# Token softmax sums kept as rows, their inverses spread through DRAM, token outputs divided on GpSimd one segment later

## The chip, the cores and the metric

One core of one Trainium2 chip runs the whole program. The metric is the device time in microseconds (us), the median of some runs of the same kernel. One more execution is taken under the profiler; all durations below come from that one.

## The reference, cut to what matters

Two layers, each an attention block A with a recurrent memory and a gated block B. The change is in A. The sequence of 2048 tokens is cut into 64 segments of 32, and each segment's first 8 output rows are the memory of the next, so the segments of a block follow one another strictly.

```python
for s in range(n_seg):                       # 64 segments, S = 2048, seg_len = 32
    h = concatenate([mem, xs])               # 8 memory rows and 32 tokens, Dm = 512
    q, k, v = (einsum('btd,dhe->bhte', h, W) for W in (Wq, Wk, Wv))   # 32 heads of 128
    scores = where(mask, einsum('bhqe,bhke->bhqk', q, k) * scale, -1e9)
    p = softmax(scores)                      # every query has its own sum over the keys
    o = einsum('bhqk,bhke->bhqe', p, v)
    o = einsum('bhte,hed->btd', o, Wo)
    mem = o[:, :M]                           # M = 8: wanted by the next segment
    outs.append(o[:, M:])                    # wanted only at the end of the block
```

The kernel works without a maximum: it takes exp of the scaled scores, multiplies by a mask of 0 and 1, and divides the product with V by the sum.

## The kernel before, in words

`a_block` (from L657) runs 64 times the function `segment` (from L891); 128 segments in the two layers. In one segment, in the order in which the code hands work to the engines:

- **Projections.** `qk` (L905) makes q and k in four chunks of 16 matmuls (L701), `v_mm` makes v in two. ScalarE casts each chunk to bf16 (L908), VectorE transposes it (L911) into `QQ` (queries) and `KA` (keys, two buffers in turn). The last 8 tokens of each segment don't depend on the memory; their q, k and v come a block of 128 tokens ahead, from the filler described below, and GpSimd copies them into `QQ` and `KX` (`prep_segment`, L864 and L867), a segment or more before they are read.
- **Scores.** `scores(r)` (L934, L938) for each half r of the heads, `exps(r)` on ScalarE (L943), `close(r)` on VectorE (L946), which multiplies `S` by the mask into `E`. Between the two, VectorE copies the second half of V out of PSUM (`VA`, L1040).
- **Sums and products.** `sums_ahead` (L969) sums the memory queries of half 0 over the keys, `pv(r)` (L986, L989) multiplies `E` by V into `psO`, `sums_memory` (L960) sums the memory queries of half 1, and `sums_tokens` (L978) those of the 32 tokens. `sums_tokens` and `sums_memory` use a matrix of ones 128 wide as weights, so that each sum stands in all 128 partitions at once: `psT` is 128 x 1024. `memory_out(r)` inverts the memory sums on ScalarE as exp(-ln) (L1003, L1004), and VectorE multiplies (L1005) into `uT`, columns 24 to 31.
- **Output projection.** `wo_pairs` (`px`, L777) and `wo_rest` (L784) multiply `uT` of this segment, 32 columns for each head, by Wo. Columns 24 to 31 are this segment's memory rows, columns 0 to 23 the first 24 token rows of the segment before: `tok_out` put them there. So the token outputs are wanted by the `px` of the next segment. The last 8 token rows go to `oB` (`last_out`) and are projected blocks later.
- **The way back.** ScalarE and VectorE copy one part of `px` (`cross`, L1065 and L873), VectorE adds (L875, L882) and transposes (L883) the memory rows into `hT`; then the next segment's projections can start.
- **Token outputs.** ScalarE inverts `psT` into `Rt` (Ln of 1024 elements, L1067, then Exp twice 512, L1070); VectorE multiplies `psO` by `Rt` in `tok_out` (L1008) and `last_out` (L1011).

The order on TensorE, VectorE and ScalarE is that of the code. GpSimd and SyncE (SP) aren't in that list: their instructions are placed by a scheduler. SP issues the DMAs and does so in order: a DMA that waits holds up those behind it.

**Filler.** `fill()` takes the next piece of work that no segment waits for: the projections of the block to come (`b_units`, L740) or the projection of finished last rows (`y_part`, L800). One unit is 16 matmuls of 512 columns; every second unit is given out in pieces, the others at once. Before the change there are three calls in a segment: one ahead of `sums_ahead` (4 matmuls), one behind it (12), and one near the segment's end (a whole unit), in front of the next projections. In the fourth segment of the first blocks no unit is left and `fill` does nothing.

**Buffers and names that the change touches:** `KAr` (L712) and the pool `a_vs` of `VA` (L679) have two buffers each; `attO` is the PSUM of `psO`, taken again by the next segment's `psK`; `att` that of `psT`, taken again by `psQ`. `spare1` (L1134) and its like hold VectorE and GpSimd work of the rows that are finished.

Of the kernel before, what the change touches and what calls it, by code (L numbers as in the profile page):

```python
# [10 lines left out]
ALU = mybir.AluOpType  # L11
# [42 lines left out]
def _consts(ctx, tc, c, b_sp):  # L54
    nc = tc.nc
    cp = ctx.enter_context(tc.tile_pool(name="consts", bufs=1))
    bsp = cp.tile([P, 16], F32, name="bsp")
    tctx = ExitStack()
    tmp = tctx.enter_context(tc.tile_pool(name="consts_tmp", bufs=1))
    ident_f = tmp.tile([P, P], F32, name="ident_f")  # L60
    nc.gpsimd.memset(ident_f[:], 0.0)
    nc.gpsimd.affine_select(out=ident_f[:], in_=ident_f[:], compare_op=ALU.not_equal, fill=1.0,
                            base=0, pattern=[[-1, P]], channel_multiplier=1)
    ident_bf = cp.tile([P, P], BF16, name="ident_bf")
    nc.vector.tensor_copy(ident_bf[:], ident_f[:])
# [24 lines left out]
    nc.vector.memset(ones[:], 1.0)  # L90
    half = cp.tile([P, 2, 32], BF16, name="half")
    nc.vector.memset(half[:], 0.0)
    for g in range(2):
        nc.vector.memset(half[64 * g:64 * g + 64, g, :], 1.0)
    bsp_bf = cp.tile([P, 16], BF16, name="bsp_bf")
# [8 lines left out]
    c.update(ident_bf=ident_bf, maskN=maskN, ones=ones, half=half)  # L104
    return c


# [374 lines left out]
def kernel(  # L482
# [30 lines left out]
    rp = ctx.enter_context(tc.tile_pool(name="rows", bufs=1))  # L513
    rows = _Rows(nc, rp, xd, xb_d, o_d, x_in)
    rows.vb_d = dram.tile([P, 8 * DH], BF16, name="vb_d")
    with tc.manual_schedule(engines=ORDERED):
        _act_table(nc)
        for tt in range(2):
# [138 lines left out]
def a_block(tc, c, rows, front, MV_in, RS_in, MV_out, RS_out, ahead, wo, S, first):  # L657
# [1 line left out]
    NSEG = S // SEG  # L659
    NB = S // P  # L660
    scale = float(DH) ** -0.5
    maskN, ones, half = c["maskN"], c["ones"], c["half"]

    with ExitStack() as ctx:

# [10 lines left out]
            KTBr[i], QTBr[i] = (a.rearrange("p (r h k) -> p r h k", r=2, h=16) for a in v[2:])  # L676
        pers = ctx.enter_context(tc.tile_pool(name="a_pers", bufs=1))
        wk = ctx.enter_context(tc.tile_pool(name="a_work", bufs=2))
        vsp = ctx.enter_context(tc.tile_pool(name="a_vs", bufs=2))  # L679
        rowp = ctx.enter_context(tc.tile_pool(name="a_rows", bufs=4))  # L680
        segp = ctx.enter_context(tc.tile_pool(name="a_seg", bufs=2))
        acc_pool = ctx.enter_context(tc.tile_pool(name="a_ps_acc", bufs=1, space=PSUM))
# [26 lines left out]

        memT = [pers.tile([P, P], BF16, name=f"memT{i}") for i in range(2)]  # L710
        NKQ = 2
        KAr = [pers.tile([P, 2, 16, 32], BF16, name=f"KA{i}") for i in range(2)]  # L712
        QQr = [pers.tile([P, 2, 16, 40], BF16, name=f"QQ{i}") for i in range(NKQ)]
        KXr = [pers.tile([P, 4, 2, 32], BF16, name=f"KX{i}") for i in range(NKQ)]
        uT = [pers.tile([P, H, 32], BF16, name=f"uT{i}") for i in range(2)]
# [24 lines left out]
        def b_units(tb, early=0):  # L740
# [59 lines left out]
        def y_part(G, q, last=False):  # L800
# [5 lines left out]
                parts = [[(groups[g], 8 * q + k) for g in range(4)] for k in range(8)]  # L806
            pwB = accA.tile([P, DM], F32, name="pwB")
            for k, _ in enumerate(wo_last(parts, pwB)):
                if k in (0, 3):
                    yield  # L810

            def add(lo, n, src):
# [43 lines left out]

        seg_state = {}
        oBs = {}

        def prep_segment(s, eng=nc.gpsimd):  # L860
            tb, j4 = s // 4, s % 4
# [29 lines left out]
        def segment(s, fill, spare1, spare2, spare3, tail, loads):  # L891
            tb, j4 = s // 4, s % 4
            st = seg_state.pop(s)
            QQ, KX, VX = st["QQ"], st["KX"], st["VX"]
            KA = KAr[s % 2]
# [76 lines left out]
            def sums_tokens(ps):  # L972

                for k in range(2):
                    for g in range(2):
# [2 lines left out]
                        nc.tensor.matmul(o[:, :, :, 24:32] if k else o, lhsT=ones[64 * g:64 * g + 64, :],  # L978
                                         rhs=e_own(e, 1) if k else e_all(e, 8, 40), start=(k == 0), stop=True, skip_group_check=True)

            def pv(r):

                for i in range(4):
# [83 lines left out]
            nc.scalar.activation(out=Rt[:], in_=psT[:], func=ACT.Ln)  # L1067
            for r in range(2):
                rt = Rt[:, :, 256 * r:256 * r + 256]
                nc.scalar.activation(out=rt, in_=rt, func=ACT.Exp, scale=-1.0)  # L1070
            run(turns)
            spare2()
            t1 = wk.tile([P, P], F32, name="t1", bufs=1)
# [10 lines left out]
            tok_out(1)  # L1084
            last_out(1)
            run(adds)
            run(turns)
            tail()
# [4 lines left out]
        if first:  # L1093
# [1 line left out]
                ln_turn(tb, nc.scalar.copy)  # L1095
            units, units1 = b_units(0, 6), b_units(1, 2)
            for gen in (units, units1, units):
                for _ in range(3):
# [13 lines left out]
            rows.y_load(y, first, nc.gpsimd, rows.pool.tile([P, DM], F32, name="y_x")[:], o)()  # L1112

        def values(units):
            for n in (2, 1):
                for _ in range(n):
                    next(units)
                run(copies)
# [152 lines left out]
```

## Time and profile before

| what | value |
|---|---|
| runs | 1626.39, 1627.11, 1627.98 us; median 1627.11 |
| profiled execution, span | 1630.2 us (no other time is given for it) |
| granted TensorE clock, mean | 0.996 |
| one ordinary segment, `scores(0)` to `scores(0)` (309.83 to 319.83) | 10.00 us |
| a segment without filler (119.48 to 129.27) | 9.79 us |
| mean distance of segments, first layer, second layer | 10.09, 10.08 us |
| `sums_tokens` (L978), one segment, from the first start to the last end | 0.44 us |
| `Rt` on ScalarE (L1067, L1070), one segment | 1.02 and 2 x 0.62 us |
| `tok_out`, `last_out` on VectorE (L1008, L1011), one segment | 2 x 0.55 and 2 x 0.28 us |
| DMA moved | 149.27 MB, 92 GB/s on the mean |

How to read it: a row of the order of time gives start, time, engine, line, operation and the tiles "out<-in", and in brackets the idle time before it with what ended it. A row's time reaches from the first start to the last end of a run of equal instructions, and for TensorE the ends are modelled; what can be compared well are the starts. "SPq" and "POOLq" are the queues on which SP and GpSimd issue DMAs.

### The profile page before, as it was taken

The page shows a single profiled execution, that of the slowest core. Times are in us where ns is not written, and L with a number is a line of the kernel's source. Part 1 is how long each engine was busy: PE and PEld are TensorE (multiplying, and loading weights), DVE is VectorE, ACT ScalarE, POOL GpSimd, SP SyncE. Part 2 cuts the span into 40 slices and gives each one's busy share as a digit, 9 for nine tenths or more (in the row PEclk, how much of TensorE's full clock was granted, in tenths as well). Part 3 has the DMA queues.
Part 4 walks back from the last instruction along what each step waited for, and adds up shares of the span by engine and source line. Part 5 has one row for each costly group of instructions (what it writes and reads, how often), then busy time and mean ns, then how long its engine had stood idle before and what let it go on. Part 6 is the DMA issues. An engine that isn't in the chain of part 4 may idle for free.

```text
span 1630.2 us, 90461 instructions
## 1 busy us (share of the span) xinstructions
PE 1575.0 (97%) x40658; PEld 962.0 (59%) x40658; DVE 1211.3 (74%) x3179; ACT 1064.1 (65%) x2278; POOL 290.2 (18%) x604
## 2 busy tenths in 40 slices
PE   4899999999999999999999999999999999999999
PEld 1456665665566556566656566666655666664565
DVE  3677777778888888884467777777888788878622
ACT  2577777777777777661047777777777777775400
POOL 5111111111211221320011111111121112224000
PEclk9899999999999999999999999999999999999999
DMA  9322122223321334387951222121233123425697
GB/s 352 105 44 43 44 44 44 43 46 75 81 56 43 79 87 84 91 182 145 214 167 48 45 50 46 46 46 46 62 97 79 46 72 95 98 55 172 141 189 162
DMA packets 264748, 149.27 MB, mean 92 GB/s; under 512 B 198680, under 2 KB 240784, under 8 KB 264360
## 3 DMA queue, kind: packets, MB, share of 16 engines
q1 hardware_dynamic: 251128, 99.66, 28.4%
q0 software_dynamic: 13232, 43.82, 8.3%
q8 instruction: 319, 5.23, 1.4%
q14 instruction: 69, 0.57, 0.1%
HBM read 59.68 MB, written 37.19 MB: 59 GB/s over the span
## 4 chain that ended last, share of the span: by engine, by line
PE 54%; DVE 1%; ACT 1%; DMA 1%; issue 0%; SPq 0%; DVEq 0%
PE pg L392 9%; PE psQ L701 7%; PE psK L701 7%; PE psb L701 5%; PE pz L291 4%; PE px L777 4%; PE psV L701 3%; PE psm L701 3%; PE psO L784 3%; PE py L435 2%; PE psO L986 2%; PE pwB L796 1%; PE psT L978 1%; PE psS L934 1%; PE pw L1223 0%; PE psO L969 0%
## 5 line engine op out<-in xcount | busy, mean ns | idle before, releaser
L701 PEld LDWEIGHTS <-hT 128*32 128x32 bf16 x12288 | 331.9, 97 | 309.2 <-DVE hT L883 65.5
L911 DVE STREAM_TRANSPOSE QQ<-rows 128x512 bf16<-128x512 bf16 x256 | 179.2, 700 | 20.2 <-ACT rows L908 13.0
L911 DVE STREAM_TRANSPOSE KA<-rows 128x512 bf16<-128x512 bf16 x256 | 176.3, 689 | 14.7 <-ACT rows L908 13.1
L908 ACT CAST rows<-psQ 128x512 bf16<-128x512 f32 x256 | 142.8, 584 | 22.7 <-PE psQ L701 21.1
L392 PE MATMUL pg<-z,wspT 128*128 128x344 bf16 x1024 | 154.3, 309 | 0.0
L1005 DVE TENSOR_TENSOR uT<-psO,Rm 128x128 bf16<-128x128 f32 x256 | 74.5, 291 | 106.7 <-PE psO L989 56.6
L1070 ACT ACTIVATE Rt<-Rt 128x512 f32<-128x512 f32 x256 | 147.3, 622 | 4.1
L1008 DVE TENSOR_TENSOR uT<-psO,Rt 128x384 bf16<-128x384 f32 x256 | 140.4, 548 | 10.8 <-ACT Rt L1070 4.1
L701 PE MATMUL psQ<-Wq_sb,hT 128*32 128x512 bf16 x2048 | 136.2, 383 | 10.2 <-ACT Rt L1067 4.4
L943 ACT ACTIVATE S<-psS 128x224 bf16<-128x224 f32 x256 | 91.4, 357 | 81.1 <-PE psS L938 81.1
L777 PEld LDWEIGHTS <-uT 128*32 128x32 bf16 x4608 | 111.6, 96 | 46.8 <-DVE uT L1005 32.7
L701 PE MATMUL psQ<-Wk_sb,hT 128*32 128x512 bf16 x2048 | 136.2, 383 | 0.0
L777 PE MATMUL px<-Wo,uT 128*32 128x256 bf16 x3840 | 135.3, 275 | 0.3 <-DVE uT L1005 0.3
L701 PE MATMUL psm<-Wq_sb,hT 128*32 128x512 bf16 x2048 | 134.9, 380 | 0.0
L701 PE MATMUL psK<-Wk_sb,hT 128*32 128x512 bf16 x2048 | 134.4, 379 | 0.0
L701 PE MATMUL psK<-Wv_sb,hT 128*32 128x512 bf16 x2048 | 134.4, 379 | 0.0
L701 PE MATMUL psV<-Wv_sb,hT 128*32 128x512 bf16 x2048 | 133.6, 378 | 0.0
L1067 ACT ACTIVATE Rt<-psT 128x1024 f32<-128x1024 f32 x128 | 131.0, 1024 | 3.1
L784 PE MATMUL psO<-Wo_high,uT 128*32 128x128 bf16 x7168 | 126.9, 220 | 5.9 <-issue 3.3
L392 PEld LDWEIGHTS <-wspT 128*128 128x128 bf16 x1024 | 100.2, 98 | 53.2
L867 POOL COPY KX<-old 128x128 bf16<-128x128 bf16 x128 | 69.1, 550 | 299.3 <-PE psS L938 224.8
L867 POOL COPY KX<-front 128x128 bf16<-128x128 bf16 x126 | 66.6, 548 | 303.9 <-PE psS L938 222.5
(194 smaller groups left out, 2908.2 us busy)
## 6 DMA issues: line engine op xcount, KB each, us to landing
o_d<-o_sb SPq DMA_DIRECT2D x126, 64.0 KB
vb_d<-front SPq DMA_DIRECT2D x30, 256.0 KB
VX<-vb_d SPq DMA_DIRECT2D x120, 64.0 KB
ln_x<-xd SPq DMA_DIRECT2D x26, 256.0 KB
y_o<-o_d POOLq DMA_DIRECT2D x22, 256.0 KB, 3.4
xd<-y_o POOLq DMA_DIRECT2D x22, 256.0 KB, 3.2
Wq_sb<-in_A_Wq_dram POOLq DMA_DIRECT2D x8, 512.0 KB, 9.7
Wk_sb<-in_A_Wk_dram POOLq DMA_DIRECT2D x8, 512.0 KB, 11.1
```

Of the source, the lines that this page charges most:

```text
L392: nc.tensor.matmul(pg[t][:, k, 0:344], lhsT=wsp[t][:, st, :], rhs=z(st, 344 * k, 344 * k + 344), start=(st == 0), stop=(st == NT - 1))
L701: return [nc.tensor.matmul(ps[32 * cg:32 * cg + 32, :], lhsT=lhs(kt, cg), rhs=rhs(kt, cg), start=(kt == 0), stop=(kt == KT - 1), tile_posi ...
L777: nc.tensor.matmul(px[at:at + 32, 0:256], lhsT=lhs[:, h, :], rhs=wo_rhs(h, slice(k + 2, None, -2) if h % 2 else slice(k, None, 2)), start= ...
L784: nc.tensor.matmul(pw[32 * cg:32 * cg + 32, :], lhsT=lhs[:, h, :], rhs=wo_rhs(h, cg), start=False, stop=(h == H - 1), tile_position=(0, 32 ...
L867: eng.tensor_copy(KX[:, :, r].rearrange("p g (k i) -> p i g k", i=4), bs["KTB"][:, r].rearrange("p (i g) k -> p i g k", i=4)[:, :, :, 8 * ...
L908: return r, mms, nc.scalar.copy(r[:], ps)
L911: nc.vector.transpose(out=QQ[:, j % 2, :, 0:32] if j < 2 else KA[:, j % 2], in_=r[:])
L943: return nc.scalar.activation(out=S[:, r], in_=psS[:, r, 0:224], func=ACT.Exp, scale=scale)
L1005: nc.vector.tensor_tensor(out=hview(uT_cur[:], r, 24, 32), in0=oview(r, 0, 8), in1=rm.rearrange("p g (n q) -> p g n q", q=8), op=ALU.mult)
L1008: nc.vector.tensor_tensor(out=hview(uT_nxt[:], r, 0, 24), in0=oview(r, 8, 32), in1=rview(r, 0, 24), op=ALU.mult)
L1067: nc.scalar.activation(out=Rt[:], in_=psT[:], func=ACT.Ln)
L1070: nc.scalar.activation(out=rt, in_=rt, func=ACT.Exp, scale=-1.0)
```

## The change

Except in the last segment of a block, where all stays as it was (`ahead_of` is false):

- `sums_rows` takes the place of `sums_tokens`: for each of four (half, key side) parts of `E`, one matmul for all keys and one for the own ones, with the weights `pick` (128 x 32: 16 equal columns of ones for each half of the partitions), in four column tiles of TensorE. Each sum then stands in 16 partitions and not in 128, and `psT` is used 128 x 128.
- ScalarE inverts these 128 x 128 (`Rr`), SP writes one partition out of each 16 to DRAM (`r_d`, 8 x 128), and two DMAs read it back, copied to all 128 partitions, into `Rt`.
- ScalarE copies `psO` (128 x 512 for each half) into `raw` in SBUF; `tok_out` and `last_out` on VectorE go.
- `norm_tokens` multiplies `raw` by `Rt` in eight products on GpSimd, four with 192 elements a partition into `uT` and four with 64 into `oB`. It is kept in `late` and handed out in the next segment, behind its token sums and ahead of its `px`.
- The divided filler unit comes in three pieces (4, 8 and 4 matmuls), and `fill` is called once more, behind the token sums.
- `KA` and `VA` have one buffer each.

Cut to its core:

```diff
-        vsp = ctx.enter_context(tc.tile_pool(name="a_vs", bufs=2))
+        vsp = ctx.enter_context(tc.tile_pool(name="a_vs", bufs=1))
-        KAr = [pers.tile([P, 2, 16, 32], BF16, name=f"KA{i}") for i in range(2)]
+        KAr = [pers.tile([P, 2, 16, 32], BF16, name="KA")]
-                for kts in (((0,), (1, 2, 3)), ((0, 1, 2, 3),))[k % 2]:
+                for kts in (((0,), (1, 2), (3,)), ((0, 1, 2, 3),))[k % 2]:
+            def sums_rows(ps):
+                for k in range(2):
+                    for q in range(4):
+                        e = E[:, q // 2, q % 2, :]
+                        rhs = e[:, 160:224].rearrange("p (i b e) -> p i b e", i=4, b=2)[:, :, 1, :] if k else heads40(e[:, 0:160])[:, :, 8:40]
+                        o = ps[32 * q:32 * q + 32, :].rearrange("p (i q) -> p i q", i=4)
+                        nc.tensor.matmul(o[:, :, 24:32] if k else o, lhsT=pick[:].rearrange("p g m -> p (g m)"), rhs=rhs,
+                                         start=(k == 0), stop=True, tile_position=(0, 32 * q), skip_group_check=True)
+            def raw_out(raw, r):
+                nc.scalar.copy(raw[:, r].rearrange("p g s i q -> p g (s i) q"), oview(r, 8, 40))
...
-            sums_tokens(psT)
+            ahead_of = s + 1 < NSEG
+            if ahead_of:
+                sums_rows(psT[:, 0, 0:P])
+            else:
+                sums_tokens(psT)
+            if late:
+                late.pop(0)()
+            if not (first and s == 0):
+                fill()
             memory_out(1, sums[1])
...
+            if ahead_of:
+                Rr = segp.tile([P, P], F32, name="Rr", bufs=1)
+                nc.scalar.activation(out=Rr[:], in_=psT[:, 0, 0:P], func=ACT.Ln)
+                nc.scalar.activation(out=Rr[:], in_=Rr[:], func=ACT.Exp, scale=-1.0)
+                r_d = rows.r_d[s % 2]
+                nc.sync.dma_start(r_d[:], Rr[:].rearrange("(a b) c -> a b c", b=16)[:, 0, :])
+                raw = segp.tile([P, 2, 2, 2, 4, 32], F32, name="raw", bufs=1)
+                rb = Rt[:].rearrange("p r (s g i q) -> p r s g i q", s=2, g=2, i=4)
+                for r in range(2):
+                    nc.sync.dma_start(Rt[:, r, :], r_d[4 * r:4 * r + 4, :].rearrange("a c -> (a c)").partition_broadcast(P))
+                    raw_out(raw, r)
+                def norm_tokens():
+                    for lo, hi in ((0, 24), (24, 32)):
+                        for r in range(2):
...
+                            for k in range(2):
+                                nc.gpsimd.tensor_tensor(out=o[:, :, k], in0=raw[:, r, :, k, :, lo:hi], in1=rb[:, r, k, :, :, lo:hi], op=ALU.mult)
+                late.append(norm_tokens)
...
-            tok_out(0)
-            last_out(0)
+            if not ahead_of:
+                tok_out(0)
+                last_out(0)
             fill()
```

More of the change, by code (lines that the diff above doesn't have):

```diff
@@ L94, in _consts @@
         nc.vector.memset(half[64 * g:64 * g + 64, g, :], 1.0)
+    pick = cp.tile([P, 2, 16], BF16, name="pick")
+    nc.vector.memset(pick[:], 0.0)
+    for g in range(2):
+        nc.vector.memset(pick[64 * g:64 * g + 64, g, :], 1.0)
     bsp_bf = cp.tile([P, 16], BF16, name="bsp_bf")
@@ L103, in _consts @@
     tctx.close()
-    c.update(ident_bf=ident_bf, maskN=maskN, ones=ones, half=half)
+    c.update(ident_bf=ident_bf, maskN=maskN, ones=ones, half=half, pick=pick)
     return c
@@ L515 @@
     rows.vb_d = dram.tile([P, 8 * DH], BF16, name="vb_d")
+    rows.r_d = [dram.tile([8, P], F32, name=f"r_d{i}") for i in range(2)]
     with tc.manual_schedule(engines=ORDERED):
@@ L661, in a_block @@
     scale = float(DH) ** -0.5
-    maskN, ones, half = c["maskN"], c["ones"], c["half"]
+    maskN, ones, half, pick = c["maskN"], c["ones"], c["half"], c["pick"]
     with ExitStack() as ctx:
@@ L808, in y_part @@
             for k, _ in enumerate(wo_last(parts, pwB)):
-                if k in (0, 3):
+                if k in (0, 2, 3):
                     yield
@@ L858, in a_block @@
         oBs = {}
+        late = []
         def prep_segment(s, eng=nc.gpsimd):
@@ L894, in segment @@
             QQ, KX, VX = st["QQ"], st["KX"], st["VX"]
-            KA = KAr[s % 2]
+            KA = KAr[0]
             VA = vsp.tile([P, 2, 4, DH], BF16, name="VA")
@@ L1066, in segment @@
             Rt = segp.tile([P, 2, 512], F32, name="Rt", tag="Rt", bufs=1)
[L1067 to L1070, printed above, removed]
+            if ahead_of:
[12 more added lines that the diff above has]
+                        for r in range(2):
+                            if lo == 0:
+                                o = uT_nxt[:, :, 0:24]
+                            else:
+                                o = oB[:, :, 8 * (s % 16):8 * (s % 16) + 8]
+                            o = o.rearrange("p (r g s i) q -> p r g s i q", r=2, g=2, s=2)[:, r]
+                            for k in range(2):
+                                nc.gpsimd.tensor_tensor(out=o[:, :, k], in0=raw[:, r, :, k, :, lo:hi], in1=rb[:, r, k, :, :, lo:hi], op=ALU.mult)
+                late.append(norm_tokens)
+            else:
+                nc.scalar.activation(out=Rt[:], in_=psT[:], func=ACT.Ln)
+                for r in range(2):
+                    rt = Rt[:, :, 256 * r:256 * r + 256]
+                    nc.scalar.activation(out=rt, in_=rt, func=ACT.Exp, scale=-1.0)
             run(turns)
@@ L1079, in segment @@
             spare3()
-            tok_out(0)
-            last_out(0)
+            if not ahead_of:
+                tok_out(0)
+                last_out(0)
             fill()
             run(copies)
-            tok_out(1)
-            last_out(1)
+            if not ahead_of:
+                tok_out(1)
+                last_out(1)
             run(adds)
@@ L1097, in a_block @@
             for gen in (units, units1, units):
-                for _ in range(3):
+                for _ in range(4):
                     next(gen)
@@ L1114, in values @@
         def values(units):
-            for n in (2, 1):
+            for n in (3, 1):
                 for _ in range(n):
```

## The prediction

> **What bounds the kernel now.** I read the page first (busy time, then the chain that ended last), then the stages by segment, then the order of time inside one segment on TensorE, VectorE and GpSimd.
>
> ```profile
> PE 1575.0 (97%) x40658; PEld 962.0 (59%) x40658; DVE 1211.3 (74%) x3179; ACT 1064.1 (65%) x2278; POOL 290.2 (18%) x604
> PE 54%; DVE 1%; ACT 1%; DMA 1%; issue 0%; SPq 0%; DVEq 0%
> ```
>
> TensorE is busy nearly throughout and carries the chain. GpSimd is nearly idle, so moving work there looks free. But a share is an average, so I compare two segments, from one `scores(0)` to the next: an ordinary one, with filler, and one for which no filler is left (fourth segment of an early block).
>
> ```profile
> 309.83:319.83 10.00, 10.00 (x310) 6.04 (x306) 7.68 (x22) 7.84 (x17) 1.09 (x3) 1.00 0.31 37
> 119.48:129.27 9.79, 8.75 (x276) 5.56 (x272) 7.91 (x22) 6.99 (x15) 1.96 (x5) 1.00 0.24 38
> ```
>
> The columns are length, then PE, PEld, DVE, ACT and POOL busy, granted clock, DMA share and GB/s. The clock is 1.00 in both. Without its filler TensorE is idle for 1.04 us, and yet the segment is only 0.21 us shorter. So a second chain, the softmax one through VectorE and ScalarE, lies 0.21 us behind TensorE, and no saving on TensorE alone is worth more than about that. The middle of an ordinary segment, on TensorE:
>
> ```profile
> 309.83 0.27 PE L934 MATMUL psS<-QQ,KA 128*32 128x40 bf16 x16
> ...
> 310.95 0.39 PE L701 MATMUL psb<-Wq_sb,hB 128*32 128x512 bf16 x4
> 311.17 0.29 PE L969 MATMUL psO<-E,half 128*32 128x64 bf16 x16
> 311.28 0.82 PE L701 MATMUL psb<-Wq_sb,hB 128*32 128x512 bf16 x12
> 312.04 0.32 PE L986 MATMUL psO<-E,VA 64*128 64x80 bf16 x8
> ...
> 312.25 0.31 PE L986 MATMUL psO<-E,VA 64*128 64x80 bf16 x8
> 312.39 0.22 PE L989 MATMUL psO<-E,VX 64*128 64x128 bf16 x2
> 312.44 0.22 PE L960 MATMUL psO<-E,ones 64*128 64x64 bf16 x4
> 312.50 0.44 PE L978 MATMUL psT<-E,ones 64*128 64x512 bf16 x4
> 312.87 0.29 PE L777 MATMUL px<-Wo,uT 128*32 128x256 bf16 x4
> ```
>
> I count from `scores(0)` at 309.83. Ends are modelled, so I use starts: `pv(1)` at +2.42, the memory sums at +2.61, the token sums at +2.67, `px` at +3.04, the second part of `px` (head 15 and on) at +3.82.
>
> **The change on TensorE.** The token sums go from 640 columns for each pair of row tiles to 160 for each set of four column tiles. Four matmuls of 512 columns take 0.22 us (310.95 to 311.17), so 640 take 0.27, and 160 take 0.07: 0.20 less. The filler between `sums_ahead` and `pv(0)` falls from 12 matmuls to 8, so `pv(0)` starts 0.22 earlier; the 4 moved ones come behind the sums. Total filler is the same. `pv(1)` can't follow all the way, for it needs the second `E` (L946). In the segment without filler, that wait gives `pv(1)` at 121.75 - 119.48 = +2.27, and from the memory sums to the second part of `px` (ScalarE's two steps and L1005) 123.16 - 121.96 = 1.20. With `pv(1)` at +2.27 and 0.21 to the memory sums, that part comes at 2.27 + 0.21 + 1.20 = +3.68, against +3.82. TensorE would be there at 2.48 + 0.06 + 0.07 + 0.22 + 0.05 for the change of tiles + 0.78 = +3.66, so the softmax chain ends last. **Gain: 0.14 us** a segment. From there on nothing is shorter: the wo, filler and projection matmuls run back to back to the next `scores(0)`. Of the 126 segments changed 8 have no filler, and are at +3.68 already: 118 x 0.14 = 16.5 us.
>
> **What leaves VectorE and ScalarE** is worth little. L1008 and L1011 (2 x 0.55 + 2 x 0.28 = 1.66 us) run in the shadow of 4.3 us of projections. ScalarE gives up 1.02 + 2 x 0.62 and takes the small Ln and Exp (about 0.28 and 0.31, by the Rm rows of the same shape) and two `raw` copies (0.58 each, by `VA`): 2.26 becomes 1.75, under the same cover. Some six segments in which VectorE runs late (`sums_ahead` at +1.45 to +1.55) may regain 0.2 each: 1 us. The single buffers of `KA` and `VA` are free: their last readers are 8 us gone.
>
> **The inverses' way.** `Rr` is ready 1.4 us after the second part of `px` (0.44 to the cross copy, 0.26, 0.28, 0.31 and gaps), at +5.1. SP then stores 4 KB and waits for it. A 4 KB store isn't shown. The first packet of the 64 KB store `o_d<-o_sb` goes 1.15 after its issue and the last ends at 2.08; the 256 KB store `vb_d` lets its reader go after 2.0 at the least. So 1.2 to 2.1; I take 1.6. The 256 KB loads, by `ln_x<-xd`, end 2.8 after issue, +0.4 to the waiter; the quickest `vb_d` suggests 2.1 in all. So the first half of `Rt` is there 3.3 to 5.3 after +5.1, which is -1.5 to +0.5 in the next segment (of 9.86); I take -0.4, the second half 0.6 later, and both 0.5 later where transposes, `VX` or `ln_x` stand ahead on SP. What waits behind these on SP (the `o_d` store, transposes) goes about 2 us later; its readers, the KX and QQ copies, run a segment or more ahead of `scores`, so that costs nothing. The same copies stand behind the products on GpSimd, with the same slack.
>
> **The products on GpSimd.** These rows give their length:
>
> ```profile
> L864 POOL COPY QQ<-old 128x256 bf16<-128x256 bf16 x64 | 25.8, 403 | 116.8 <-DMA old<-rowsB 67.1 <-PE psS L938 20.5 <-PE psm L701 14.5
> L624 POOL COPY hB<-hT 128x128 bf16<-128x128 bf16 x30 | 8.9, 296 | 139.4 <-DMA hT<-ln_xn 135.9 <-ACT Rt L1070 3.5
> L223 POOL TENSOR_TENSOR y_o<-y_o,y_x 128x512 f32<-128x512 f32 x4 | 4.9, 1214 | 9.8 <-DMA y_o<-o_d 9.8
> ```
>
> The copies give 0.18 fixed; the sum of 512 then 2.0 ns an element. So 192 elements take 0.57 and 64 take 0.31: 4 x 0.57 + 4 x 0.31 = 3.5 us a segment, beside 1.1 to 2.0 now. In the built program's order the two halves alternate (wide, wide, narrow, narrow, twice). The last wide one ends 2.9 after the first half lands: +2.5 by my value, and it is due at about +3.9. So `px` isn't held up, with a margin of 1.4, less the waits below.
>
> **The price is the port.** The products run from -0.4 to +3.1, and both `E` (L946, two SBUF inputs, due at +0.80 and +1.82) fall inside. A copy on GpSimd that starts just ahead of `E` delays it, and one behind it is delayed:
>
> ```profile
> 1266.82 0.48 POOL L867 COPY KX<-old 128x128 bf16<-128x128 bf16 x1 [8.22 <-DMA old<-rowsB]
> 1266.86 0.49 DVE L946 TENSOR_TENSOR E<-S,maskN 128x448 bf16<-128x448 bf16 x1
> ...
> 321.67 0.69 POOL L867 COPY KX<-old 128x128 bf16<-128x128 bf16 x1
> ```
>
> `E` alone takes 0.38 and the copy 0.47. At 1266.86 `E` is 0.11 longer, so 128 elements held it for 0.15 from their start; a QQ copy of 256 at 1127.60 made an `E` 0.03 later 0.23 longer. That is 1 ns an element of one input; two inputs at 2 ns give 0.39 for a wide product and 0.13 for a narrow one. An `E` at a random moment of the wide pairs waits (0.39 / 0.57) x 0.195 = 0.13 on the mean, 0.39 at most; in the narrow pairs 0.03, 0.13 at most. Both waits count: `VA`'s copy stands between the two `E` (it starts as the first ends, and the second starts as it ends), and `pv(1)` waits for the second. Bounds: 0 to 0.78 a segment. I take 0.18, between one wide and two wide collisions. Net 0.18 - 0.14 = +0.04, by 118: 5 us. L1005 (one SBUF input) keeps its 0.29 beside the 1.2 us sums on GpSimd, so other VectorE work doesn't pay.
>
> The Trainium skill says more (SBUF — State Buffer, "Who interferes with whom"): the first to start holds the shared pair for its whole instruction. The trace differs: the KX copy of 300.35 to 300.82 leaves the `E` that starts at 300.64 at 0.39.
>
> **Smaller terms.** The block's last segments put sums of 1.2 us and DMA issues of 0.54 ahead of the products: about 1 us twice. 64 MB more of DMA may slow TensorE's code loads: 0 (the early segments, with hardware DMA alone, show 10.00) to 0.08 a segment (the mean excess over 10.00 now), so 0 to 10 us; I take 0. Sum: -16.5 + 21 + 2 - 1 = +5.5. Against the profiled execution (span 1630.2, 0.2% above the median of the runs) that is 1635.7; on the median of 1627.11 it is **1632**.
>
> **Rivals.**
> 1. *The gain comes whole.* The wide products fall clear of both `E`, or hold the port for less than worked out. For it: GpSimd leaves gaps of 0.18 between them. Against: 2.3 us of wide products beside two `E` 1.0 apart. -16 to -10: 1611 to 1617.
> 2. *The inverses come late* (slower). It decides once the first half lands after +0.6: 0.6 + 2.9 + 0.4 of waits for `E` = +3.9. Each 0.1 beyond costs 0.1 in all 118 segments. Landing at +0.9 to +1.2 costs 35 to 70: 1662 to 1697. [...] Against: the rows allow +0.5 at the most on a quiet queue.
> 3. *The port is held for the whole product.* Then `E` waits 0.28 on the mean in wide pairs and 0.15 in narrow ones, 0.43 in all, and 0.43 - 0.14 = 0.29 by 118 is +34: 1661. The row at 300.64 speaks against it. It is what the rule of the Trainium skill above (SBUF — State Buffer) would make of these rows.
> 4. *TensorE's saving does nothing*, because the softmax chain already bounds the segment: the segments without filler, at 9.79, exclude it for the ordinary ones.
>
> **How the numbers follow.** A measurement can tell about 0.2% (3.3 us) from no change. Forecast 0.45, rival 1 0.28, rival 2 0.15, rival 3 0.12, rival 4 nothing. The forecast's own range is 1620 to 1643 (mean waits of 0.08 to 0.27): below 1623.8 lie 0.07 of its 0.45, within 0.2% 0.14, above 0.24. Faster is 0.28 + 0.07 = 0.35, same 0.14, slower 0.24 + 0.27 = 0.51. The range takes in rivals 1 and 3 and the nearer end of 2: 1609 to 1668.
>
> **What will show it.** TensorE step: `psT<-E,pick` in about 0.1 us, `pv(0)` 0.2 earlier, and the second part of `px` at +3.68 where `E` is undisturbed. Port: `E` with a mean over 0.45 in place of 0.39, where a product started just ahead. Inverses: `px` waiting for VectorE and not for GpSimd; if for GpSimd, rival 2. It is wrong if `E` stays at 0.39 (rival 1), or if `px` stands behind GpSimd.

## The result and the profile after

The changed kernel takes 1778.0 us (median, 1775.9 to 1784.2) where the one before, measured beside it, took 1627.6: a ratio of 1.0921 (95% interval 1.0897 to 1.0945), 150 us slower. Forecast were 1632, in a range of 1609 to 1668. Below, the excess of a kernel is its ratio less one, times 1627, so that kernels measured at different times can be set side by side.

The page of the changed kernel, busy times and the chain that ended last:

```profile
PE 1616.4 (91%) x41139; PEld 945.6 (53%) x41162; DVE 1090.1 (61%) x2678; ACT 1016.6 (57%) x2404; POOL 704.6 (40%) x1612
...
PE 58%; DMA 14%; ACT 8%; DVE 7%; POOL 7%; issue 4%; SPq 0%; POOLq 0%; DVEq 0%; ACTq 0%
PE psQ L706 11%; PE psK L706 9%; PE pg L396 8%; DMA Rt<-r_d 7%; PE px L782 5%; PE psm L706 5%; DMA r_d<-Rr 4%; PE pz L295 4%; POOL uT L1117 4%; ACT raw L1025 4%; DVE E L952 3%; PE psV L706 2%; PE psb L706 2%; PE py L439 2%; PE psO L1002 2%
```

TensorE falls from 97% to 91%, and the chain now leaves it for the DMAs of the inverses, `raw`, the products and `E`. Two segments, as windows with the same columns as before:

```profile
339.97:350.71 10.74, 10.20 (x314) 5.94 (x309) 6.63 (x17) 7.45 (x18) 4.54 (x11) 1.00 0.40 101
372.30:382.90 10.60, 10.21 (x312) 6.08 (x308) 7.18 (x20) 7.93 (x20) 4.66 (x12) 1.00 0.41 115
```

Neither is an outlier: over 125 segments the mean distance went from 10.08 to 11.25 us, the median to 11.02. By parts (means): `scores(0)` to the second part of `px` 3.84 before, 4.09 after; from there to `psQ` 1.91 before, 2.80 after; `psQ` to the next `scores(0)` 4.34 and 4.35. So three quarters of the loss lie in a stretch that the prediction passed over. In the second segment nothing disturbs the first part; its TensorE rows (start, length, operation):

```profile
372.30 0.27 PE L940 MATMUL psS<-QQ,KA 128*32 128x40 bf16 x16
...
374.29 0.32 PE L1002 MATMUL psO<-E,VA 64*128 64x80 bf16 x8
...
374.92 0.26 PE L994 MATMUL psT<-E,pick 128*32 128x128 bf16 x8
375.02 0.39 PE L706 MATMUL psb<-Wq_sb,hB 128*32 128x512 bf16 x4
375.23 1.04 PE L782 MATMUL px<-Wo,uT 128*32 128x256 bf16 x30
376.00 0.41 PE L782 MATMUL px<-Wo_high,uT 128*32 128x256 bf16 x6
```

The row sums hold TensorE 0.10, `pv(0)` is 0.22 earlier (+1.99) and the second part of `px` stands at +3.70. The saving is there; the segment is 0.6 longer all the same. Why shows in the other one, 339.97, between `px` and `psQ`, on VectorE, ScalarE and TensorE:

```profile
344.76 0.29 DVE L881 TENSOR_TENSOR t<-px,cross 128x128 f32<-128x128 f32 x1
345.82 0.23 DVE L888 TENSOR_TENSOR memT<-psO,t 128x64 bf16<-128x64 f32 x1 [0.76 <-ACT raw L1025]
346.08 0.25 DVE L889 STREAM_TRANSPOSE hT<-memT 128x64 bf16<-128x64 bf16 x1
```

```profile
344.97 0.31 ACT L1098 ACTIVATE Rr<-Rr 128x128 f32<-128x128 f32 x1
345.20 1.07 ACT L1025 COPY raw<-psO 128x512 f32<-128x512 f32 x2
```

```profile
344.14 0.97 PE L789 MATMUL psO<-Wo_high,uT 128*32 128x128 bf16 x56
344.92 1.05 PE L706 MATMUL psb<-Wk_sb,hB 128*32 128x512 bf16 x16
346.38 0.83 PE L706 MATMUL psQ<-Wq_sb,hT 128*32 128x512 bf16 x12 [0.41 <-DVE hT L889]
```

`memT` needs `pw`, done at 345.11, and `t`, done at 345.05. It starts at 345.82, when the first copy to `raw` is over. This copy reads other columns of the PSUM tile in which `pw` lies. `memT` and the copy only read the tile, but in the built program `memT` waits for ScalarE, where before the change it waited for TensorE. The Trainium skill has the rule (PSUM — Partial Sum Buffer, "PSUM bank collisions raise a hardware error"): the compiler's back end puts a dependency between any two instructions on different engines that touch one bank and quadrant, reads among them. The trace agrees that one reader waits for the other; which tool put the wait there isn't seen. VectorE's lists of waits before and after (us in total, times, longest):

```profile
DVE memT L882 <- PE psO L784: 10.4, 21, 2.7
```

```profile
DVE memT L888 <- ACT raw L1025: 117.7, 124, 3.5
```

It waits 124 times in 126 segments, 0.95 on the mean. The filler covers a part; `psQ` waits 57 us for `hT` (1.2 before).

### The profile page after: what moved, and what is told of

Its sections match the earlier page's. It is cut to its first block, busy times and chain, and to the rows that moved or that the text cites. A ratio compares the mean times of both kernels' runs of the same rounds, so it can differ in the third digit from the quotient of the medians.

```text
span 1778.0 us, 92860 instructions
## 1 busy us (share of the span) xinstructions
PE 1616.4 (91%) x41139; PEld 945.6 (53%) x41162; DVE 1090.1 (61%) x2678; ACT 1016.6 (57%) x2404; POOL 704.6 (40%) x1612
## 4 chain that ended last, share of the span: by engine, by line
PE 58%; DMA 14%; ACT 8%; DVE 7%; POOL 7%; issue 4%; SPq 0%; POOLq 0%; DVEq 0%; ACTq 0%
PE psQ L706 11%; PE psK L706 9%; PE pg L396 8%; DMA Rt<-r_d 7%; PE px L782 5%; PE psm L706 5%; DMA r_d<-Rr 4%; PE pz L295 4%; POOL uT L1117 4%; ACT raw L1025 4%; DVE E L952 3%; PE psV L706 2%; PE psb L706 2%; PE py L439 2%; PE psO L1002 2%
## 5 line engine op out<-in xcount | busy, mean ns | idle before, releaser
L1117 POOL TENSOR_TENSOR uT<-raw,Rt 128x192 bf16<-128x192 f32 x504 | 303.2, 621 | 640.8 <-DMA Rt<-r_d 452.0
L706 PEld LDWEIGHTS <-hT 128*32 128x32 bf16 x12288 | 309.3, 97 | 405.7 <-DVE hT L889 145.8
L914 ACT CAST rows<-psQ 128x512 bf16<-128x512 f32 x256 | 150.0, 586 | 129.9 <-PE psQ L706 129.8
L917 DVE STREAM_TRANSPOSE KA<-rows 128x512 bf16<-128x512 bf16 x256 | 182.0, 711 | 40.7 <-ACT rows L914 33.8
L782 PEld LDWEIGHTS <-uT 128*32 128x32 bf16 x4608 | 119.6, 96 | 63.8 <-POOL uT L1117 32.5
L789 PE MATMUL psO<-Wo_high,uT 128*32 128x128 bf16 x7168 | 136.7, 222 | 12.4 <-issue 6.7
L1025 ACT COPY raw<-psO 128x512 f32<-128x512 f32 x252 | 135.3, 589 | 20.4 <-PE psO L789 13.9
L952 DVE TENSOR_TENSOR E<-S,maskN 128x448 bf16<-128x448 bf16 x256 | 128.5, 502 | 15.0 <-ACT S L949 0.6
L789 PEld LDWEIGHTS <-uT 128*32 128x32 bf16 x7168 | 117.7, 98 | 21.6 <-issue 12.4
L888 DVE TENSOR_TENSOR memT<-psO,t 128x64 bf16<-128x64 f32 x252 | 51.6, 205 | 117.9 <-ACT raw L1025 117.7
```

The costliest lines, as they stand in the source:

```text
L706: return [nc.tensor.matmul(ps[32 * cg:32 * cg + 32, :], lhsT=lhs(kt, cg), rhs=rhs(kt, cg), start=(kt == 0), stop=(kt == KT - 1), tile_posi ...
L782: nc.tensor.matmul(px[at:at + 32, 0:256], lhsT=lhs[:, h, :], rhs=wo_rhs(h, slice(k + 2, None, -2) if h % 2 else slice(k, None, 2)), start= ...
L789: nc.tensor.matmul(pw[32 * cg:32 * cg + 32, :], lhsT=lhs[:, h, :], rhs=wo_rhs(h, cg), start=False, stop=(h == H - 1), tile_position=(0, 32 ...
L914: return r, mms, nc.scalar.copy(r[:], ps)
L917: nc.vector.transpose(out=QQ[:, j % 2, :, 0:32] if j < 2 else KA[:, j % 2], in_=r[:])
L952: nc.vector.tensor_tensor(out=E[:, r], in0=S[:, r].unsqueeze(1).to_broadcast([P, 2, 224]), in1=maskN[:], op=ALU.mult)
```

## The experiments

**1. `raw` behind `memT`.**

```diff
-                    raw_out(raw, r)
+                    if r:
+                        raw_out(raw, r)
...
                 build_hA(s + 1, pw, t1)
+            if ahead_of:
+                raw_out(raw, 0)
             if s > 0:
                 store_o(s, pw, t1)
```

> One edit to the changed kernel: the second copy of raw (first half of psO, the tile that also holds pw) is issued behind memT, so that VectorE's memT no longer waits for ScalarE. Theory (two causes side by side: 0.76 us a segment of 1.17 is memT behind raw, the rest is lateness of the inverses, the port and code loads): the memT wait goes from 118 us to near nothing, and 0.3 to 0.75 us a segment comes back, less than all because a shorter segment leaves the inverses less time: 1685 to 1740. Rival A (one loop sets the segment: px, Rr, the way through DRAM, the products, px again; the raw wait only fills time that would pass anyway): no gain beyond 15 us, 1763 or more, and px waits longer for GpSimd instead. Rival B (slower code loads because of more DMA): also no gain, with the waits of PE's sequencer unchanged.

1756.9; ratio 1.0783 (1.0750 to 1.0816), excess 127, so only 23 less. The wait for `raw` is gone, and a part is given back elsewhere, on TensorE:

```profile
PE px L782 <- POOL uT L1118: 36.2, 40, 4.3
```

It was 16.0 in 24 before this edit. A missed number: neither the theory's 38 to 93 nor rival A's nothing.

The granted clock has a part in it. In this run's trace nine segments hold a stretch of 3.4 or 6.8 us at a clock of 0.50, 34 us in all; in the changed kernel's three do (10 us), in those of runs 2, 3 and 6 none. Each of these stretches comes behind a wait of 1.2 to 4.3 us of `px` for the products. One of them, as a window and on TensorE:

```profile
1284.10:1290.90 6.80, 5.66 (x116) 3.45 (x120) 1.81 (x8) 2.09 (x6) 3.96 (x10) 0.50 0.23 40
```

```profile
1285.24 2.01 PE L782 MATMUL px<-Wo,uT 128*32 128x256 bf16 x30 [2.98 <-POOL uT L1118]
...
1288.74 1.92 PE L706 MATMUL psb<-Wk_sb,hB 128*32 128x512 bf16 x16
```

The 16 projection matmuls take 1.92 there and 1.05 at 344.92 above. The nine segments take 14.6 on the mean, the other 116 take 10.8. If half of each such stretch is lost, an estimate from these rows, the clock takes 17 us here and 5 in the changed kernel, and so hides some 12 us of what this edit is worth.

**2 and 3. Products by a constant** in place of `Rt`, the DMAs kept; then both edits together.

```diff
-                                nc.gpsimd.tensor_tensor(out=o[:, :, k], in0=raw[:, r, :, k, :, lo:hi], in1=rb[:, r, k, :, :, lo:hi], op=ALU.mult)
+                                nc.gpsimd.tensor_tensor(out=o[:, :, k], in0=raw[:, r, :, k, :, lo:hi], in1=const[:, :, :, lo:hi].to_broadcast([P, 2, 4, hi - lo]), op=ALU.mult)
```

> The changed kernel with products by a constant tile in place of Rt; the DMAs stay, so the token outputs are not divided by their sums (that part of the computation is left out). The products no longer wait for the inverses, and run ahead of E. Theory: the memT wait stays (0.76 x 126 = 95), the lateness and the E price go: 1627 + 95 - 16 + code loads = 1705 to 1735. Rival A (the loop through DRAM sets it all): 1610 to 1640. Rival B (DMA traffic): 1760 or more.

> The edits of the two runs before it together (products by a constant, division left out; raw of the first half behind memT), DMAs kept. Theory: only the TensorE saving of 0.14 a segment and the cost of the DMA traffic are left: 1611 to 1630. Rival B: 1720 or more. If it lands between, what is left is the cost of the traffic or of the filler's new places.

1740.1 (1.0671, 1.0643 to 1.0698), excess 109; and 1686.0 (1.0340, 1.0320 to 1.0361), excess 55. The first misses the theory's 1735 by 5 us, the second lies between the theory (1611 to 1630) and rival B (1720 or more). With the inverses out of play, moving `raw` is worth 54 (109 to 55); with them it was 23: the two hide behind each other. And 55 remain with neither. TensorE's weight loads of the third kernel wait for nothing that the profile shows:

```profile
PEld L706 <- issue: 29.4, 53, 2.9
PEld L791 <- issue: 27.2, 34, 2.1
```

and its matmuls at 456.89 likewise:

```profile
456.11 0.28 PE L791 MATMUL psO<-Wo_high,uT 128*32 128x128 bf16 x5
456.89 0.91 PE L791 MATMUL psO<-Wo_high,uT 128*32 128x128 bf16 x51 [0.50 <-issue]
```

**4. Inverses early.** Ln and Exp of `Rr`, the store and the two loads are moved up from behind `cross` to ahead of `px`; `raw` of half 0 stays behind `memT`.

```diff
             memory_out(1, sums[1])
+            if ahead_of:
+                Rr = segp.tile([P, P], F32, name="Rr", bufs=1)
+                nc.scalar.activation(out=Rr[:], in_=psT[:, 0, 0:P], func=ACT.Ln)
+                nc.scalar.activation(out=Rr[:], in_=Rr[:], func=ACT.Exp, scale=-1.0)
...
             run(copies)
             px = accB.tile([P, 512], F32, name="px")
```

> The changed kernel, whole computation: Ln and Exp of the rows of sums and the DMA way stand ahead of the cross copy on ScalarE (directly behind memory_out), some 1.2 us earlier, and raw of the first half goes behind memT. Theory: products start at about -0.6 instead of +0.56 and px isn't held; left are the E price (0.22 a segment) less the TensorE saving (0.14) and some late segments: 1632 to 1670. Rival A gives the same here if the loop is made 1.2 us shorter (1630 to 1660), so this run tells only whether the inverses can be made timely. Rival B: 1740 or more.

1740.7 (1.0687, 1.0630 to 1.0744), excess 112: far above the theory's 1632 to 1670, and at rival B's 1740 or more. Beside the first experiment the exp ends 1.7 earlier (+4.2 for +5.9), the products start 1.1 earlier (-0.01 for +1.06), and `px` waits for them 10 us and not 36. Yet only 15 us come back, and the waits for nothing that the profile shows, on TensorE's two rows (weight loads and matmuls, added up, though they overlap in part), rise from 112 to 155 us. So something besides lateness and `memT` is at work.

**5. The filler alone**, in the kernel before (8 matmuls ahead of `pv(0)`, 4 behind the full sums).

> The kernel before with one part of the change alone: the filler in three places (8 matmuls ahead of pv(0), 4 behind the full token sums). Theory: TensorE brings px at about +3.12 instead of +3.04 and nothing else moves, 4 to 10 us: 1630 to 1640. Rival C (the filler's new places, more changes between weights and column tiles, cost what is left over in the run with constant products): 1660 or more.

1633.7 (1.0048, 1.0033 to 1.0063), excess 8; `px` at +3.12 as forecast. Rival C falls.

**6. Both edits, without store and loads.**

```diff
-                nc.sync.dma_start(r_d[:], Rr[:].rearrange("(a b) c -> a b c", b=16)[:, 0, :])
...
-                    nc.sync.dma_start(Rt[:, r, :], r_d[4 * r:4 * r + 4, :].rearrange("a c -> (a c)").partition_broadcast(P))
```

> The run with both edits (constant products, raw of the first half behind memT; division left out) without the store to r_d and the two loads to Rt; Ln and Exp of the row sums stay. Theory, revised after the first four runs (four causes: memT behind raw, lateness of the inverses, the port, and 64 MB of DMA that slow TensorE's code loads; the waits for nothing that the profile shows rose from 31 to 116 us on TensorE's two rows): most of the 56 us that this pair of edits left goes, 1615 to 1640, and the issue waits fall under 50 us. Rival C (the new places of the filler, the copies of raw, or GpSimd's products as such): 1670 or more.

1639.8 (1.0083, 1.0064 to 1.0102), at the end of the expected 1615 to 1640, excess 13 (of 55). The DMAs, which nobody waits for in either, cost 42. The weight loads' waits fall too:

```profile
PEld L706 <- issue: 16.7, 35, 2.9
PEld L791 <- issue: 10.4, 17, 2.1
```

On TensorE's two rows together 48 us for 116; with what overlaps counted once, and within the segments, 34 for 78; on the matmul row alone 8 for 33. The page lists a queue that carries instructions, here of the changed kernel (packets, MB, share):

```profile
q8 instruction: 323, 5.29, 1.3%
```

These are 323 packets of 16 KB, one for every 255 of the 82301 instructions on TensorE's two rows. In run 3 the matmul row has 45 waits of this kind over 0.25 us, 31 us in all, and 44 of them end 1 to 2 us after such a packet has landed (9 would by chance), nearly all 1.25 to 1.6 us after; without the DMAs there are 14, 8 us, and all 14 do. So TensorE runs out of code, which comes late beside the loads. This is a coincidence in time plus an on-off test; where the packet is held up wasn't seen, and a packet's own transfer is as long in all runs (1.06 to 1.15 us). Of the 42 us, 24 stand in these waits of the matmul row; its waits for `hT` (14 for 9) and for `E` (8 for 6) grow too, and how the rest comes about isn't shown.

**7 and 8. The loads alone, in the kernel before** (with one buffer of `KA` and `VA`). First with nothing that paces them (from `x_in`, without the store), then as in this edit, with a store like the changed kernel's ahead of them.

```diff
+                nc.sync.dma_start(r_d[:], cross[:].rearrange("(a b) c -> a b c", b=16)[:, 0, :])
+                for r in range(2):
+                    nc.sync.dma_start(scratch[r][:], r_d[4 * r:4 * r + 3, :].rearrange("a c -> (a c)").partition_broadcast(P))
```

> The kernel before, whole computation, plus two broadcast loads of 192 KB a segment from DRAM into a scratch tile that nobody reads (three quarters of the bytes of the changed kernel's loads; KA and VA have one buffer, as in the changed kernel, to make room). Nothing waits for these loads but the next ones. Theory with code loads: three quarters of 45 to 60 us, 1658 to 1680, issue waits of TensorE 80 us or more. Rival C: 1627 to 1640.

> The kernel before, whole computation, with the changed kernel's DMA pattern: each segment stores 4 KB of cross to r_d and then loads it twice, broadcast, into scratch (192 KB each, three quarters of the changed kernel's bytes), so the loads can't run ahead as they did in the run before. Nobody waits for them but the next segment's. Theory: three quarters of the 46 us that the DMAs cost with constant products, 1650 to 1670, and TensorE's waits for nothing that the profile shows 80 us or more. If the traffic costs nothing in itself: 1627 to 1636.

The first took 1845.7 (1.1348, 1.1330 to 1.1366), beyond any theory, and tests nothing: SP ran ahead by up to 55 segments, the loads of many segments stood in the queues at once, and VectorE waited 140 us in 13 places for the `o_d` store behind them. The second: 1653.6 (1.0156, 1.0113 to 1.0199), as expected, excess 25 (18 to 32) for three quarters of the bytes (42 would give 31), with 61 us of issue waits on the two rows (31 before; 80 were expected).

**9. Half the bytes:** early inverses with `r_d` and `Rt` in bf16; and **10.** `raw` in bf16 too.

> The run with the inverses made early (1740.7) with r_d and Rt in bf16: half the bytes of the loads (128 KB each), the same number of DMAs and products. Theory with code loads by bytes: 20 to 30 us come back, and the shorter loads land a little earlier: 1695 to 1722. If the number of DMAs or packets decides and not their bytes: 1730 to 1745. If a product with a bf16 input is shorter, E is held for less too, a few us.

> The run with early inverses and bf16 loads (1713.5), with raw in bf16 too: the same products with two bf16 inputs, the whole computation. Theory: if the port is held by the bytes that GpSimd reads, products and E get shorter (E from 0.49 towards 0.45, 10 us) and the products end earlier: 1695 to 1710. If elements decide: 1710 to 1716.

1713.5 (1.0541, 1.0521 to 1.0561), excess 88, 24 less than in float32 and as expected: the bytes count, and it is the quickest version with the whole computation. By which way isn't separated: the issue waits of the two rows fall from 155 to 106 us, all `E` together from 130.8 to 125.3. With `raw` in bf16 1727.8 (1.0597, 1.0557 to 1.0636), above both expectations: no gain, a wide product takes 0.573 in place of 0.575 (0.621 with both in float32). Why it was slower is open (12 us more of issue waits on the weight loads).

**11 and 12. The port alone:** products without inverses held back until beside `E`, no DMAs. The first try put a one-column copy of `KA` ahead of the products; the second, below, makes their factor from `QQ`.

```diff
+                    nc.gpsimd.tensor_copy(const[:, 0, 0, :], QQ[:, 1, 0, 0:32])
```

> The run with constant products and no DMAs (1639.8), with a one-column copy of KA on GpSimd ahead of the products, so that they start at about +0.5 after scores(0) and stand beside both E, as in the changed kernel, but never wait for inverses (division left out). Theory: the port alone, 0.18 to 0.25 us a segment: 1662 to 1675, E from 0.42 to about 0.5 on the mean; px may wait a little for the last wide product. Then of the 71 us between this pair of kernels (raw behind memT, with inverses or with constants) some 45 are lateness. If the port is nearly free: 1640 to 1648; if lateness is small and the port carries it: 1695 or more.

> The run with constant products and no DMAs (1639.8), where the factor is now copied on GpSimd from QQ of the same segment (transposed just ahead of scores(0)), ahead of the products, so that they can't start before about +0.2 after scores(0) and stand beside both E. (In the run before it the copy had been scheduled behind the products on GpSimd, which still started at -3; it did not test this.) The division is left out. Theory: E goes from 0.42 to 0.55 on the mean, 0.25 to 0.35 us a segment: 1668 to 1690, px not held for more than 0.1. If the port is nearly free: 1640 to 1650.

The first (1645.1; 1.0094, 1.0067 to 1.0120) is a failed test: the scheduler put the copy behind the products. The second: 1675.7 (1.0263, 1.0244 to 1.0282), as expected, excess 43, 30 over the sixth run; `E` there:

```profile
L953 DVE TENSOR_TENSOR E<-S,maskN 128x448 bf16<-128x448 bf16 x256 | 130.3, 509 | 14.7 <-ACT S L950 0.4
```

130.3 for 106.1 us: 24 of the 30 are `E` made longer.

**13. The same with the DMAs.**

> The run before (products gated by QQ, beside both E, constant in place of inverses, raw of the first half behind memT) with the store to r_d and the loads to Rt put back; the division is left out. It differs from the first experiment (1756.9) only in that the products never wait for the inverses. Theory (DMA 46 and port with gate 36 add up): 1639.8 + 46 + 36 = 1722, 1710 to 1732, so lateness itself is 25 to 45 us. If DMA and port share their cover, 1690 to 1708, and lateness is 50 or more; if they aggravate each other, 1740 or more, and lateness is almost nothing.

1789.6 (1.0957, 1.0939 to 1.0975), no quicker than the changed kernel. It isn't the difference that I wanted: in 29 segments the products now stand behind a copy on GpSimd that waits over 1 us for a transpose, which SP issued late, behind `r_d`:

```profile
394.06 0.45 POOL L874 COPY KX<-front 128x128 bf16<-128x128 bf16 x1 [7.64 <-DMA front<-rowsB]
394.32 0.21 POOL L1110 CAST const<-QQ 128x32 f32<-128x32 bf16 x1
394.62 2.23 POOL L1119 TENSOR_TENSOR uT<-raw,const 128x192 bf16<-128x192 f32 x4
```

Those segments take 13.6, the others 10.8, and 18 of the 29 hold a stretch at half clock. In the changed kernel and in experiment 1 no first product stands behind such a copy. That led me to sort experiment 1 by what SP issues in the 4.5 us ahead of the store:

| ahead of `r_d` on SP (experiment 1) | segments | products start | next segment |
|---|---|---|---|
| nothing of these | 36 | +0.39 | 10.71 |
| `hT` transpose, `ln_x` | 25 | +0.96 | 10.84 |
| transposes | 31 | +0.60 | 10.99 |
| `VX` loads and a transpose | 27 | +2.70 | 12.12 |

One of the last kind, on SP:

```profile
406.74 1.75 SPq L735 DMA_DIRECT2D VX<-vb_d  x4
408.59 1.25 SPq L772 DMA_TRANSPOSE old<-rowsB  x1
409.95 0.60 SPq L1100 DMA_DIRECT2D r_d<-Rr  x1
414.04 1.29 SPq L1104 DMA_DIRECT2D Rt<-r_d  x2
```

The loads go 4.1 us after the store, not 1.9. Over 10.71, these classes lose 3 + 9 + 38 = 50 us. Six of the nine segments with half clock are in the last class, whose median is 11.43. That class isn't long by its place in the block: in run 3, with the same DMAs, its segments take 10.48, those of the first class 10.52. In the changed kernel all four classes lie between 11.20 and 11.36; there the products of the last one start at +1.42.

**14 and 15. `VX` loads off SP**, in experiment 1 and in the quickest version. The loads also move one segment later, except in the first block of the first layer.

```diff
-                nc.sync.dma_start(bs["VX"][q:q + 32]...
+                nc.gpsimd.dma_start(bs["VX"][q:q + 32]...
...
-                if j4 == 1 + 2 * (first and tb == 0) and tb + 1 < NB:
+                if j4 == 2 + (first and tb == 0) and tb + 1 < NB:
```

> The first experiment (whole computation, raw of the first half behind memT, 1756.9) with the four VX loads of each block issued by GpSimd instead of SP. There, SP stood at the VX loads and their wait for vb_d ahead of the store to r_d in one segment of four, the products of that segment started 2.59 after scores(0) (0.2 to 0.5 in segments without them), and the segment took 12.15 in place of 10.7. Theory: that class of segments falls to about 10.8, 32 x 1.3 = 43 us: 1700 to 1725. If the late start comes from the loads' traffic and not from SP's order: 1745 or more. The four issues of about 0.55 on GpSimd may cost up to 0.5 in a segment (10 us).

> The best whole computation so far (inverses early, r_d and Rt in bf16, 1713.5) with the VX loads issued by GpSimd. Theory: its segments behind VX loads are hardly later than the others (P0 -0.48 against -0.6), so little comes back: 1700 to 1712, still slower than the kernel before, because the E price (0.2 a segment), the DMAs (some 23 us) and the filler's places stay.

1735.3 (1.0658, 1.0634 to 1.0681), excess 107, 20 less, with the `VX` class gone; the 59 segments behind transposes are at 11.13. Half of what was expected: behind transposes the store goes out in time (0.08 late on the mean), but its loads follow 2.6 after it, where 1.95 pass with nothing ahead. The run doesn't tell the other queue from the later place. On the early version nothing: 1716.4 (1.0544, 1.0510 to 1.0578).

**The sum, each step with its runs:**

| | us |
|---|---|
| filler's places, products and `raw` copies as such, less the TensorE saving (run 6; filler alone 8) | 13 |
| store and loads beside TensorE's code (3 less 6; 24 of it seen as late code) | 42 |
| late inverses and the port (1 less 3) | 72 |
| `memT` behind `raw` (after less 1; 54 alone) | 23 |

These add to 150 by construction. Of the 72, `E` is longer by 22.5 us in experiment 1 than in 3, and SP's classes give 50, with the half clock (an estimated 17) for the most part inside them. That split rests on the traces; the run meant to measure it (13) did not.

## Why the prediction was wrong

- **"From there on nothing is shorter"**, and the `raw` copies "under the same cover": this step failed. I priced the copies by ScalarE's time and not by what they read. `psO[0]` holds `pw`, so the copy stands between `wo_rest` and `memT`, on the way that sets the segment. Worth 54 us alone, 23 in company.
- **DMA traffic, "0 to 10 us; I take 0"**: 42. I read it from early segments of the kernel before, at 43 to 44 GB/s; the changed one runs at 82 to 89 there. The bound was no bound, because no row had code and this traffic together.
- **The inverses' way**: mechanism seen (rival 2, with its point at +0.6 and 35 to 70 us; about 50 measured), sizes too small (the 50 are SP's classes of experiment 1). `Rr` was done at +5.6 (5.1), SP was late by 0.39 on the mean, store to loads took 2.26 (1.6; bounds 1.2 to 2.1), loads to products 3.64 (2.8; bounds 2.1 to 3.2): 11.9 for 9.5. The products started at +0.56 for -0.4, and not later still, only because the segment had grown. That late products also bring the half clock (34 us of it in experiment 1) was in no term. Small errors of one sign in four links, and "0.5 later" where SP has other work was 1.4 behind the `VX` loads (2.3 in experiment 1).
- **"so that costs nothing"** for what waits on SP behind the store: nothing speaks against it in the changed kernel. In 13, with another order on GpSimd, such a copy held up the products in 29 segments.
- **TensorE's step** was right: +3.70 where undisturbed (3.68), and 3.71 on the median in run 6. There the quickest tenth of the segments takes 9.88 (9.99 before), the median one 9.95 (10.01). But 0.11 a segment is 14 us at best, and run 6 as a whole is 13 slower. The 0.05 for the change of tiles has no row of its own; from the row sums to `px` 0.31 passed, for 0.34 in the sum.
- **The port** was right in kind: `E` at 502 ns (over 450 forecast), 28 us in all (21 forecast). Wide products take 621 (570), narrow ones 349 (310), by the page and the list of groups:

```profile
L1117 POOL TENSOR_TENSOR uT<-raw,Rt 128x192 bf16<-128x192 f32 x504 | 303.2, 621 | 640.8 <-DMA Rt<-r_d 452.0
...
L952 DVE TENSOR_TENSOR E<-S,maskN 128x448 bf16<-128x448 bf16 x256 | 128.5, 502 | 15.0 <-ACT S L949 0.6
```

- **Rival 3** (held for the whole product) falls. An `E` that started 0.03 behind a wide product took 0.82; one that started 0.46 behind a wide product, which ran on for 0.14, took its usual 0.39:

```profile
329.43 0.82 DVE L952 TENSOR_TENSOR E<-S,maskN 128x448 bf16<-128x448 bf16 x1
...
351.51 0.39 DVE L952 TENSOR_TENSOR E<-S,maskN 128x448 bf16<-128x448 bf16 x1
```

  The others lie between: an `E` that starts t behind a wide product is longer by 0.45 - t, behind a narrow one by 0.18 - t (0.39 and 0.13 in the prediction). So the port is held for 0.45 of 0.59, and for 0.18 of 0.32. The rule of the Trainium skill that I cited (SBUF — State Buffer, "Who interferes with whom") says the whole instruction, and says it of VectorE's two-port modes; of an operation like `E`, with two SBUF inputs, it says that it contends with a GpSimd instruction that reads SBUF, and not for how long. The measured hold is shorter than the recorded length, and the measurement decides.
- **Rival 1** was taken in by all this; nothing of a whole gain was seen.

## What to carry to other kernels

Before moving a reader, look at which PSUM tile it reads and who else reads it next: a copy that is "only ScalarE time" can stand between a matmul and the step that sets the loop. A value sent through DRAM has to be counted link by link with the queue it stands in, at the busiest segment and not the mean, and its traffic priced against the code that TensorE fetches. When two causes hide behind each other, take them away singly and together (23, 41, and 95 for both), or the first experiment looks like a refutation.

## What the runs showed of the hardware that was not expected

- Two broadcast loads of 256 KB in every 10 us, waited for by nobody, cost 42 us in 1640. The waits of TensorE's matmuls for nothing that the profile shows rose from 8 to 33 us with them, and 44 of the 45 longest ended 1 to 2 us after a 16 KB packet of instructions had landed.
- A GpSimd product of 192 elements took 0.621 with two float32 inputs, 0.575 with one and 0.573 with none: half the bytes shorten it by 8% at most (0.588, 0.549 and 0.547 on the median, clear of any `E`).
- Behind waits of TensorE of 1.1 to 4.3 us for late products, the granted clock fell to 0.50 for 3.4 or 6.8 us, in nine segments of experiment 1 and in 22 of run 13. Not every such wait was followed by one: experiment 1 has 23 waits of matmuls over 1 us in its segments.
- A 4 KB store let its dependent loads go 1.72 us after its issue at the quickest tenth, 1.99 at the median, and 4.1 behind four 64 KB loads on the same queue.
